# One core, a convolution and dense pair with its gradients: w1's gradient summed with the operands exchanged, products with w2 and the first norm moved forward

## The chip, the cores and the metric

The kernel runs on one core of a Trainium2 chip. Its engines work side by side, each in the order of its own queue: TensorE (PE; its weight loads are shown as PEld), VectorE (DVE), ScalarE (ACT), GpSimd (POOL) and SyncE (SP). Transfers are issued by an engine's queue, mostly SP's and POOL's, and carried out by 16 DMA engines. The metric is the time of one execution on the device in microseconds; the median over runs is compared.

## The reference

Four layers in a row, each on the layer norm of its input `x` (2048 rows of 448), each added to `x`: a long convolution (A), a dense pair (B), A again, B again. All nine results are wanted: the output and the gradients of it for the given `grad_out`.

```python
def _A_ref(q, k, v, shift_k, ssm_k, ssm_D):
    k_shift = ...            # 4 taps along the rows
    kv = k_shift * v
    y_f = rfft(kv, 2*S) * rfft(ssm_k, 2*S)
    y = irfft(y_f)[:S]
    return q * (y + kv * ssm_D)

def _B_ref(x, w1, w2):       # w1 448 x 1792, w2 1792 x 448
    return silu(x @ w1) @ w2

x = A_q
x = x + _A_ref(_layernorm(x), ...)
x = x + _B_ref(_layernorm(x), B_w1, B_w2)
x = x + _A_ref(_layernorm(x), ...)
x = x + _B_ref(_layernorm(x), B_w1, B_w2)
_out, _vjp = jax.vjp(_f, A_q, A_k, A_v, A_shift_k, A_ssm_k, A_ssm_D, B_w1, B_w2)
return (_out, *_vjp(grad_out))
```

Since `y` depends on `k`, `v` and the filter alone, both A layers share one convolution. The gradient of w1 (output 7) is the sum over the 2048 rows, and over both B layers, of the norm that went in (`n3` for the second layer, `n1` for the first) times the gradient at the hidden layer.

## The kernel before

The program has three stages.

*Opening* (`_ssm_prefix`). The filter's spectrum and that of `kv` are made by two stages of 128-wide matmuls. In the loop over `h` and `jq` TensorE convolves the taps (`conv`, `ps_cv`), ScalarE copies `ks`, VectorE multiplies by `v`, and `stage1_kv` makes the first stage of the transform; beside it run the transposes of the filter (`turn`, when `h` is 0) and its second stage (`_fft_stage2` with `cons_ka`, when `h` is 1). `_ln_steps` is a generator: it makes the first norm of chunk 0, one `bn_stats` and `bn_aggr` for each of four row tiles with a `yield` after each, then in one go the reciprocal root on POOL (`rstd`, L279) and four products on ScalarE (`na`, L285). Its last part stands behind the loop (`for _ in ln0: pass`). Then 14 transfers on POOL swap the halves of the filter's spectrum into `KB`, seven more store the spectrum, and SP loads w1. Seven `turn`s transpose the first stage of `kv` (`A1kv` into `A1K`), 16 blocks of 128 x 128 each, copied by ScalarE or VectorE as the balancer `bal` picks. Then, for each of 14 pieces of 1024 columns, `_fft_stage2` and `cons_prod`: two matmuls, a copy (`xs`), the product with the spectrum on VectorE (`pab`, L471), and two pieces later the inverse stage (`ps_v`, 16 matmuls of 128 columns, L235 and L236) and its copy into `B1`. At the end 16 transposes of `gb0` (the first 512 rows of `grad_out`), a copy to `k.gT0`, and eight steps `ps_y` that give `Ysb`, the convolution `y`.

*Main*. Four chunks of 512 rows go through the layers and back. `H` is the product with w1 (`ps_h`), `O` with w2 (`ps_o`), `G` the product of a gradient with w2 transposed (`ps_g`), `N` that with w1 transposed and the norm's gradient (`ps_n`). TensorE's order is the one in which the program issues (`tc.manual_schedule`); strings such as `"OGGOGGOTOT"` in `weave` and `steps` write it out, one letter a step. `G` and `H` make 7 steps of two blocks each through `_products`: 56 matmuls of 512 columns, of which 12 have only 64 contracted rows and stand in pairs, one on each half of the array's rows, since 448 is three and a half times 128. `G` of chunk 0 (`g20`) and of chunk 1 (`g21`) for the last layer need only `grad_out` and so can be issued at any time; before, `g20` makes three steps in the opening of Main and four after the first norms of layer three, `g21` three there and four within chunk 1's `O`.

*Suffix* (`_ssm_suffix`), with `Jobs` issued between its steps. The suffix makes the gradients of the convolution. `Jobs` makes those of w2 and w1 from operands that Main has stored in DRAM (`OP_d`): `load` brings one tile of 128 hidden columns and 2048 rows (`dstat`, 512 KB), `group` sums over 16 row tiles and two layers, and `run(n)` issues n quarters of that. For w1 (`fin_w1`, 14 tiles):

```python
# mms, L995: st is the tile of the hidden layer's gradient, mov the norm
self.nc.tensor.matmul(ps[:, :D], lhsT=st[:, t, :], rhs=mov[:, t, :], ...)
```

So the hidden gradient is stationary, the norm's 448 columns stream, and the sum comes out as 128 hidden columns x 448. Output 7 is 448 x 1792, so `fin_w1` copies the sum (L1104) and `flush`, called one block later, turns it in four transposes (`ps_dt`, L1117), copies it (L1119) and stores it from POOL (L1120).

## Time and profile before

| what | value |
|---|---|
| median of 3 runs | 717.25 us (716.99 to 719.49) |
| the profiled execution | 716.31 us |
| its span, first to last instruction | 714.5 us |
| mean granted TensorE clock | 0.995 |
| TensorE's stretch of w1's sums (`n3m` from 531.9, `n1m` to 662.8) | 448 matmuls in 131 us, with the suffix's between them |
| the first stop of TensorE over 3 us | 66.6 to 70.25 us |

The busy time of an engine is its instructions' time, laid over each other where they overlap; a matmul's recorded length is from its issue to its end, and the next one starts well before that. The price of a matmul in a stream is the distance between the starts. The 40 slices are 17.9 us each; `PEclk` is the clock granted to TensorE, in tenths.

### The profile page before, as it was taken

To read this page: it belongs to the slowest core of one execution; us is meant where nothing else is said; L and a number is where in the kernel's file an instruction comes from. 1 tells how busy PE (TensorE), PEld (TensorE's weight loads), DVE (VectorE), ACT (ScalarE), POOL (GpSimd) and SP (SyncE) were. 2 spreads that over 40 slices of the span, in tenths; PEclk is the share of its full clock that TensorE was granted. 3 is DMA by queue.
4 is the path that set the end of the run, shared out by engine and by line. 5 is a ranking of instruction groups with operands and counts; after the bars stand their busy time and mean duration, and the time that the engine had idled before them with its cause. 6 is when DMAs were issued, how large, how long until landed. Compare 5 with 4: busy or idle time off the path is not lost.

```text
span 714.5 us, 12786 instructions
## 1 busy us (share of the span) xinstructions
PE 689.3 (96%) x5008; PEld 380.9 (53%) x5008; DVE 486.2 (68%) x1106; ACT 444.2 (62%) x582; POOL 123.3 (17%) x208
## 2 busy tenths in 40 slices
PE   6997899999999999999999999999999999999998
PEld 4886654434444444444444444544566666656655
DVE  4788776758887747877279723934258769869790
ACT  3878877686777868778677685132755555545200
POOL 1034420111011100111001100001212223353130
PEclk9999899999999999999999999999999999999999
DMA  9949998659969999499975999089999897879962
GB/s 303 305 146 234 342 287 255 168 139 270 236 146 235 215 240 242 116 243 231 224 179 133 233 229 365 3 187 249 309 413 357 291 343 245 266 274 377 354 181 95
DMA packets 196237, 172.59 MB, mean 242 GB/s; under 512 B 143090, under 2 KB 174194, under 8 KB 195024
## 3 DMA queue, kind: packets, MB, share of 16 engines
q1 hardware_dynamic: 181280, 115.30, 61.3%
q0 software_dynamic: 13344, 52.54, 20.9%
q10 hardware_dynamic: 1552, 3.94, 1.5%
q8 instruction: 39, 0.64, 0.4%
q14 instruction: 22, 0.18, 0.1%
HBM read 73.25 MB, written 60.10 MB: 187 GB/s over the span
## 4 chain that ended last, share of the span: by engine, by line
PE 62%; issue 8%; DVE 5%; ACT 4%; DMA 3%; POOL 2%; POOLq 0%; DVEq 0%; ACTq 0%
PE ps_d L995 12%; PE ps_n L741 12%; PE ps_h L513 11%; PE ps_g L513 10%; PE ps_o L695 7%; PE ps_d L1030 3%; ACT dT L688 2%; DMA ksf<-KS_d 1%; PE ps_t L580 1%; PE ps_gK L1305 1%; PE ps_tr L1211 1%; POOL rstd L279 1%; PE ps_d L1065 1%; PE ps_s L206 1%; DVE n L287 1%
## 5 line engine op out<-in xcount | busy, mean ns | idle before, releaser
L995 PEld LDWEIGHTS <-dstat 128*128 128x128 bf16 x768 | 72.5, 98 | 61.1
L513 PE MATMUL ps_h<-nT,w1sb 128*128 128x512 bf16 (+1 forms) x448 | 97.4, 380 | 2.6 <-ACT dT L678 1.9
L741 PE MATMUL ps_n<-w1T,ghT 128*128 128x448 bf16 x448 | 92.5, 353 | 0.8 <-DVE ghT L866 0.8
L695 PE MATMUL ps_o<-w2sb,aT 128*128 128x448 bf16 x448 | 88.5, 352 | 0.0
L513 PE MATMUL ps_g<-nT,w2T 128*128 128x512 bf16 (+1 forms) x392 | 82.9, 380 | 0.1
L723 ACT CAST ghT<-ps_g 128x512 bf16<-128x512 f32 (+1 forms) x74 | 54.1, 760 | 41.5 <-PE ps_g L513 41.2
L673 ACT ACTIVATE aT<-ps_h 128x512 bf16<-128x512 f32 (+1 forms) x82 | 60.0, 759 | 29.2 <-PE ps_h L513 27.6
L513 PEld LDWEIGHTS <-w1sb 128*128 128x128 bf16 (+1 forms) x448 | 35.5, 97 | 59.7 <-issue 25.4
L741 PEld LDWEIGHTS <-ghT 128*128 128x128 bf16 x448 | 43.2, 98 | 42.3 <-DVE ghT L866 1.7
L695 PEld LDWEIGHTS <-aT 128*128 128x128 bf16 x448 | 43.5, 98 | 40.1
L513 PEld LDWEIGHTS <-w2T 128*128 128x128 bf16 (+1 forms) x448 | 35.4, 97 | 55.1 <-issue 20.8
L915 DVE SCALAR_TENSOR_TENSOR lb_v<-lb_u,n 128x448 bf16<-128x448 bf16 x48 | 30.0, 624 | 46.8 <-ACT lb_u L745 46.3
L279 POOL TENSOR_TENSOR rstd<-ln_ve,mhalf 128x2 f32<-128x2 f32 (+2 forms) x27 | 23.0, 851 | 198.8 <-DVE ln_ve L277 198.8
L688 ACT ACTIVATE dT<-dT 128x1024 bf16<-128x1024 bf16 (+1 forms) x64 | 55.0, 940 | 0.1
L995 PE MATMUL ps_d<-n1m,dstat 128*128 128x448 bf16 x224 | 48.6, 352 | 0.0
L995 PE MATMUL ps_d<-n3m,dstat 128*128 128x448 bf16 x224 | 48.6, 352 | 0.0
L678 ACT CAST dT<-ps_h 128x1024 bf16<-128x1024 f32 (+1 forms) x50 | 42.8, 872 | 0.0
L745 ACT ACTIVATE lb_u<-ps_n,rstd 128x448 bf16<-128x448 f32 x32 | 20.7, 647 | 34.5 <-PE ps_n L741 26.3
L995 PE MATMUL ps_d<-X,dstat 128*128 128x448 bf16 x160 | 34.2, 353 | 0.0
L995 PE MATMUL ps_d<-go,dstat 128*128 128x448 bf16 x160 | 33.7, 353 | 0.0
L581 ACT COPY nT<-ps_t 128x1024 bf16<-128x1024 bf16 x20 | 20.2, 1008 | 18.7 <-PE ps_t L580 18.7
L866 DVE TENSOR_TENSOR ghT<-dT,ghT 128x512 bf16<-128x512 bf16 (+2 forms) x24 | 18.1, 778 | 19.2 <-ACT ghT L723 17.0
(217 smaller groups left out, 1245.1 us busy)
## 6 DMA issues: line engine op xcount, KB each, us to landing
dstat<-g_d SPq DMA_DIRECT2D x28, 512.0 KB, 5.6
dstat<-a_d SPq DMA_DIRECT2D x23, 512.0 KB, 7.1
a_d<-turned SPq DMA_DIRECT2D x16, 512.0 KB, 4.1
g_d<-turned SPq DMA_DIRECT2D x16, 512.0 KB, 3.9
a_d<-turned SPq DMA_DIRECT2D x16, 384.0 KB, 3.3
g_d<-turned SPq DMA_DIRECT2D x16, 384.0 KB, 3.3
N_d<-n POOLq DMA_DIRECT2D x10, 448.0 KB, 4.6
spec_K<-ZK POOLq DMA_DIRECT2D x7, 512.0 KB, 7.7
```

The source lines that it names most:

```text
L279: k.ln_pow = nc.gpsimd.tensor_tensor(out=r[:, lo:hi], in0=ve[:, 0:n], in1=k.mhalf[:, 0:n], op=ALU.pow)
L513: nc.tensor.matmul(ps(u, u + 1)[:, 0, :], lhsT=wT[h, b, ft * P:(ft + 1) * P], rhs=rhs[h, b, :], start=start, stop=stop)
L673: self.last_silu = nc.scalar.activation(aT[hh][:, o:o + hi - lo, :], ps(lo, hi), ACT.Silu)
L678: nc.scalar.copy(self.dpart(dT, 2 * fp + lo, 2 * fp + hi), ps(lo, hi))
L688: self.nc.scalar.activation(d[:, o:o + n, :], d[:, o:o + n, :], ACT.Derivative_silu)
L695: nc.tensor.matmul(po[:, :D], lhsT=aT[ft // 7][:, ft % 7, tl * P:(tl + 1) * P], rhs=self.w2sb[:, ft, :], start=(ft == 0), stop=(ft == NF - 1))
L723: nc.scalar.copy(g, ps(lo, hi))
L741: nc.tensor.matmul(pn[:, :D], lhsT=gh[ft // 7][:, ft % 7, tl * P:(tl + 1) * P], rhs=self.w1T[:, ft, :], start=(ft == 0), stop=(ft == NF - 1))
L745: nc.scalar.activation(u0[:], pn[:, :D], ACT.Identity, scale=k.rstd[2 * L + 1][:, t:t + 1], accum_out=cp[:, tl, 0:1])
L915: nc.vector.scalar_tensor_tensor(out=v[:], in0=u0, scalar=-1.0 / D, in1=n_t, op0=ALU.mult, op1=ALU.mult, accum_out=cp[:, 1:2])
L995: self.nc.tensor.matmul(ps[:, :D], lhsT=st[:, t, :], rhs=mov[:, t, :], start=(first and t == 0), stop=(last and t == NT - 1))
L1030: nc.tensor.matmul(ps[ft][:, :D], lhsT=get(t), rhs=mov[:, t, :], start=ft not in seen, stop=(last[ft] == i and t == hi - 1))
```

## The change

`pair` takes the place of `group`, `fin_w1` and `flush` for w1: it makes two tiles of hidden columns at once, with the norm as the stationary operand and the hidden gradient's 128 columns streaming, so that the sums come out as output 7 wants them. The 448 norm columns are three blocks of 128 and one of 64; the 64-column block of the two tiles goes to the two halves of the array's columns and of one PSUM bank (`ps[0][64 * u:64 * u + 64, 384:512]`). For each row tile it issues block 0 for both tiles, the two narrow ones, and blocks 1 and 2 for both tiles: eight matmuls of 128 columns. It yields after every two row tiles, eight times a layer and pair as before. Each tile's sum is copied once and stored in two transfers. The call to `go2` moves from `group` to the last pair.

In the opening the transposes of `gb0` come before the products with the spectrum; their result lies partly in `gb0`'s own place and partly in `X`. Three steps of chunk 0's `G` (`g_step`) are issued at pieces 6 and 10 and after the last, into `k.gh0`, which lies in the rows of `X` of chunks 2 and 3; `Main.G` takes the same generator on. In Main the patterns change so that `g20` makes its four other steps before the first `H`, and `g21` its seven after the first norms of layer three; chunk 1's `"OGGOGGOTOT"` then finds no `G` step left. `gh0` serves again as the first half of chunk 0's other `G`. `_ln_steps` yields once more, after `rstd`; its steps are taken when `h` is 0 and the rest when `h` is 1. Two of the filter's second-stage pieces move to the end of `h` = 0. The `turn`s of `kv` get a fixed engine, ScalarE for g of 0, 3 and 6. w1's three loads move from SP to POOL, behind the stores of the filter's spectrum, and the memset of `w2T` to the end of the loop.

```diff
@@ -277,6 +277,7 @@
         k.ln_pow = nc.gpsimd.tensor_tensor(out=r[:, lo:hi], in0=ve[:, 0:n], in1=k.mhalf[:, 0:n], op=ALU.pow)
+        yield
         if eng is nc.scalar:
@@ -364,11 +365,11 @@
-        def turn(src, dst, g):
+        def turn(src, dst, g, eng=None):
             pt = psum.tile([P, 16, P], BF16, name="ps_tr", **a_)
...
                 nc.tensor.transpose(pt[:, i, :], src[:, 16 * g + i, :], k.ident[:])
-            _copy(nc, bal.pick(2048, dve_ns=0.53), dst[:, 16 * g:16 * g + 16, :], pt[:])
+            _copy(nc, eng or bal.pick(2048, dve_ns=0.53), dst[:, 16 * g:16 * g + 16, :], pt[:])
@@ -432,11 +433,13 @@
                             turn(A1Kf, Z, g)
+                    next(ln0)
+                    if i == 3:
+                        _fft_stage2(k, Z, psum, cons_ka, range(2))
                 else:
-                    _fft_stage2(k, Z, psum, cons_ka, range((0, 4, 8, 11)[i], (4, 8, 11, 14)[i]))
+                    _fft_stage2(k, Z, psum, cons_ka, range(2 + 3 * i, 5 + 3 * i))
                     next(ln0, None)
-        for _ in ln0:
-            pass
+        nc.gpsimd.memset(k.w2T[0:64, 3, 0:2 * P], 0.0)
         for i in range(7):
@@ -444,9 +447,9 @@
         k.w1sb = k.wk.tile([P, ND, F], BF16, name="w1sb", tag="WB")
-        nc.sync.dma_start(out=k.w1sb[:, 0:3, :], in_=k.B_w1[0:384].rearrange("(c p) f -> p c f", p=P))
-        nc.sync.dma_start(out=k.w1sb[64:128, 3, :], in_=k.B_w1[384:448, :])
-        nc.sync.dma_start(out=k.w1sb[0:64, 3, 2 * P:], in_=k.B_w1[320:384, 2 * P:])
+        nc.gpsimd.dma_start(out=k.w1sb[:, 0:3, :], in_=k.B_w1[0:384].rearrange("(c p) f -> p c f", p=P))
+        nc.gpsimd.dma_start(out=k.w1sb[64:128, 3, :], in_=k.B_w1[384:448, :])
+        nc.gpsimd.dma_start(out=k.w1sb[0:64, 3, 2 * P:], in_=k.B_w1[320:384, 2 * P:])
         nc.gpsimd.memset(k.w1sb[0:64, 3, 0:2 * P], 0.0)
@@ -455,18 +458,46 @@
         for g in range(7):
-            turn(A1f, Zkv, g)
+            turn(A1f, Zkv, g, nc.vector if g % 3 else nc.scalar)
+        bal.reset()
         hold = []
+        k.X = k.wk.tile([P, NT, D], BF16, name="X", tag="WX")
+        Xf = k.X[:].rearrange("p t d -> p (t d)")
+        k.gh0 = Xf[:, 8 * D:].rearrange("p (a s) -> p a s", s=512)
+        pt = psum.tile([P, ND, 512], BF16, name="ps_t", tag="A", bufs=4)
+        for b, (lo, hi) in enumerate(BLK):
+            for tl in range(4):
+                nc.tensor.transpose(pt[:, b, tl * P:(tl + 1) * P], k.gb0[:, tl, lo:hi], k.ident[:])
+        g3 = k.gb0[:].rearrange("p t d -> p (t d)")[:, 0:1536].rearrange("p (b s) -> p b s", s=512)
+        g1 = Xf[:, 4 * D:4 * D + 512].rearrange("p (b s) -> p b s", s=512)
+        nc.vector.tensor_copy(g3, pt[:, 0:3])
+        nc.vector.tensor_copy(g1, pt[:, 3:4])
+        bal.add("dve", 1.3)
+        class Sets:
+            def __getitem__(self, at):
+                h, b, cols = at
+                return g3[h, b, cols] if b < 3 else g1[h, 0, cols]
+        def banks():
+            ps = psum.tile([P, 2, 512], FP32, name="ps_g", tag="A", bufs=4)
+            return lambda lo, hi: ps[:, lo:hi, :]
+        k.banks = banks
+        k.g20 = _products(nc, lambda: k.banks(), k.w2T, Sets())
+        def g_step():
+            fp, ps = next(k.g20)
+            _copy(nc, bal.pick(1024), k.gh0[:, 2 * fp:2 * fp + 2, :], ps(0, 2))
...
             if ci % 2 == 1:
-                st = nc.gpsimd.dma_start(out=k.SPEC_d["KV"][:, (ci - 1) * 1024:(ci + 1) * 1024], in_=Zf[:, (ci - 1) * 1024:(ci + 1) * 1024])
-            if ci == 3:
-                with tc.issue_after(st.ins):
-                    nc.gpsimd.memset(k.w2T[0:64, 3, 0:2 * P], 0.0)
+                nc.gpsimd.dma_start(out=k.SPEC_d["KV"][:, (ci - 1) * 1024:(ci + 1) * 1024], in_=Zf[:, (ci - 1) * 1024:(ci + 1) * 1024])
             pab = work.tile([P, 2, 1024], BF16, name="pab", tag="pab", bufs=3)
@@ -474,19 +505,13 @@
                 _fft_inv_stage2_chunk(k, pa, pb, False, B1, cj, psum)
+            if ci in (6, 10):
+                g_step()
         _fft_stage2(k, Zkv, psum, cons_prod)
-        k.X = k.wk.tile([P, NT, D], BF16, name="X", tag="WX")
-        k.gT0 = k.X[:].rearrange("p t d -> p (t d)")[:, 11 * D:11 * D + 2048].rearrange("p (b t) -> p b t", b=ND)
+        g_step()
         for pa, pb, cj in hold:
             _fft_inv_stage2_chunk(k, pa, pb, False, B1, cj, psum, halves=cj == NCI - 1)
-        pt = psum.tile([P, ND, 512], BF16, name="ps_t", tag="A", bufs=4)
-        for b, (lo, hi) in enumerate(BLK):
-            for tl in range(4):
-                nc.tensor.transpose(pt[:, b, tl * P:(tl + 1) * P], k.gb0[:, tl, lo:hi], k.ident[:])
-        nc.vector.tensor_copy(k.gT0, pt[:])
         B1v = B1.rearrange("p a (c n s) -> p a c n s", c=2, n=16)
@@ -701,12 +726,18 @@
-    def G(self, gT, res, dT=None, dv=()):
+    def G(self, gT, res, dT=None, dv=(), first=None):
         nc, k = self.nc, self.k
         half = lambda h: self.t([P, NF // 2, 512], f"ghT{h}", "T", 5)
-        res[:] = [half(0)]
+        res[:] = [half(0) if first is None else first]
+        if gT is None:
+            k.banks = lambda: self.banks("ps_g")
+            prods = k.g20
+        else:
+            prods = _products(nc, lambda: self.banks("ps_g"), self.w2T, gT)
         gh = res
-        for fp, ps in _products(nc, lambda: self.banks("ps_g"), self.w2T, gT):
+        for fp, ps in prods:
             if fp == 3:
@@ -807,13 +838,13 @@
         gh2 = []
-        g20 = self.G(k.gT0, gh2, dv=(2,))
+        g20 = self.G(None, gh2, dv=(5,), first=k.gh0)
...
-        steps("GGtttG", G=g20, t=self.T2(self.n0[0][1], nT))
+        steps("GGtttGG", G=g20, t=self.T2(self.n0[0][1], nT))
         gb = gb_load(0)
@@ -825,8 +856,8 @@
         g21 = self.G(gT, gh21)
-        steps("GGGG", G=g20)
         next(g20, None)
+        steps("GGGG", G=g21)
         nT = self.nT()
@@ -883,7 +914,7 @@
                 self.fwd1(c + 1, [self.chain] * 4)
-                g = self.G(gT, gh1, dT0)
+                g = self.G(gT, gh1, dT0, first=None if c else k.gh0)
                 if c:
@@ -1009,8 +1039,6 @@
             yield from self.mms(ps[ft], st, movs[0](), 0, NT, True, False)
-        if fts == (12, 13):
-            self.go2()
         for ft in fts:
@@ -1044,9 +1072,8 @@
         movs = (lambda: self.n3, self.n1)
-        for f in range(12):
-            yield from self.group((f,), wkeys, movs, self.fin_w1)
-        yield from self.group((12, 13), wkeys, movs, self.fin_w1)
+        for i in range(NF // 2):
+            yield from self.pair(i, wkeys, movs)
         for f in range(7, 13):
@@ -1096,28 +1122,40 @@
         nc.scalar.copy(o[:], ps[:, :D])
-        self.flush()
         (nc.gpsimd if ft < NF - 2 else nc.sync).dma_start(out=k.outs[8][ft * P:(ft + 1) * P, :], in_=o[:])
-    def fin_w1(self, ft, ps):
-        o = self.out()
-        self.nc.scalar.copy(o[:], ps[:, :D])
-        self.flush()
-        self.pend = (ft, o)
-    def flush(self):
+    def pair(self, i, keys, movs):
         nc, k = self.nc, self.k
-        if self.pend is None:
-            return
-        ft, o = self.pend
-        self.pend = None
-        out7v = k.outs[7].rearrange("(c p) f -> p c f", p=DC)
-        pt = k.psum.tile([DC, ND, P], BF16, name="ps_dt", tag="tr", bufs=1)
-        for dc in range(ND):
-            nc.tensor.transpose(pt[:, dc, :], o[:, dc * DC:(dc + 1) * DC], k.ident[:])
-        o7 = k.dp3.tile([DC, ND, P], BF16, name="do7", tag="do7", bufs=2)
-        nc.scalar.copy(o7[:], pt[:])
-        nc.gpsimd.dma_start(out=out7v[:, :, ft * P:(ft + 1) * P], in_=o7[:])
+        fts = (2 * i, 2 * i + 1)
+        ps = [self.bank(tag) for tag in (("jb", "tr") if i % 2 else ("po", "po"))]
+        for L in range(2):
+            st = [self.load(keys[L], ft) for ft in fts]
+            n = movs[L]()
+            for t in range(NT):
+                last = L == 1 and t == NT - 1
+                for b in range(3):
+                    cols = slice(b * P, (b + 1) * P)
+                    for u in range(2):
+                        nc.tensor.matmul(ps[u][:, cols], lhsT=n[:, t, cols], rhs=st[u][:, t, :], start=(L == 0 and t == 0 and b == 0), stop=(last and b == 2))
+                    if b == 0:
+                        for u in range(2):
+                            nc.tensor.matmul(ps[0][64 * u:64 * u + 64, 384:512], lhsT=n[:, t, 384:D], rhs=st[u][:, t, :], start=False, stop=False)
+                if t % 2:
+                    yield 1
+            if L == 0 and i == NF // 2 - 1:
+                self.go2()
+        out = k.outs[7]
+        for u, ft in enumerate(fts):
+            o = k.dp3.tile([P, 4, P], BF16, name="dout", tag="do7", bufs=2)
+            if u == 0:
+                o0 = o
+            m = 4 - u
+            nc.scalar.copy(o[:, 0:m, :], ps[u][:, 0:m * P].rearrange("p (b f) -> p b f", f=P))
+            cols = slice(ft * P, (ft + 1) * P)
+            nc.gpsimd.dma_start(out=out[0:384, cols].rearrange("(b p) f -> p b f", p=P), in_=o[:, 0:3, :])
+            nc.gpsimd.dma_start(out=out[384:D, cols], in_=o0[64 * u:64 * u + 64, 3, :])
```

More of the change, by code (lines that the diff above doesn't have):

```diff
@@ L1098, in fin_w2 @@
         nc.scalar.copy(o[:], ps[:, :D])
-        self.flush()
         (nc.gpsimd if ft < NF - 2 else nc.sync).dma_start(out=k.outs[8][ft * P:(ft + 1) * P, :], in_=o[:])
-    def fin_w1(self, ft, ps):
-        o = self.out()
-        self.nc.scalar.copy(o[:], ps[:, :D])
-        self.flush()
-        self.pend = (ft, o)
-    def flush(self):
-        nc, k = self.nc, self.k
-        if self.pend is None:
-            return
-        ft, o = self.pend
-        self.pend = None
-        out7v = k.outs[7].rearrange("(c p) f -> p c f", p=DC)
-        pt = k.psum.tile([DC, ND, P], BF16, name="ps_dt", tag="tr", bufs=1)
-        for dc in range(ND):
-            nc.tensor.transpose(pt[:, dc, :], o[:, dc * DC:(dc + 1) * DC], k.ident[:])
-        o7 = k.dp3.tile([DC, ND, P], BF16, name="do7", tag="do7", bufs=2)
-        nc.scalar.copy(o7[:], pt[:])
-        nc.gpsimd.dma_start(out=out7v[:, :, ft * P:(ft + 1) * P], in_=o7[:])
+    def pair(self, i, keys, movs):
+        nc, k = self.nc, self.k
+        fts = (2 * i, 2 * i + 1)
[26 more added lines that the diff above has]
+            nc.gpsimd.dma_start(out=out[384:D, cols], in_=o0[64 * u:64 * u + 64, 3, :])
```

## The prediction

> **What bounds the kernel now.** I read the busy table and the 40 slices first, then the groups by line and form, the chain of waits, busy times by stretch, and last the timeline around single places.
>
> ```profile
> span 714.5 us, 12786 instructions
> PE 689.3 (96%) x5008; PEld 380.9 (53%) x5008; DVE 486.2 (68%) x1106; ACT 444.2 (62%) x582; POOL 123.3 (17%) x208
> PEclk9999899999999999999999999999999999999999
> ```
>
> TensorE is busy 96% of the span, at full clock but for the fifth slice. So what a change does to TensorE's own work is paid one for one, except in the few places where TensorE stands still. Those lie in the opening, here in the timeline of TensorE and then of ScalarE (start, length, count at the end):
>
> ```profile
> 65.14 1.46 PE L217 MATMUL ps_s<-A1K,Gsb 128*128 128x512 bf16 x6
> 70.25 0.29 PE L235 MATMUL ps_v<-Gsb,pab 128*128 128x128 bf16 x1 [3.65 <-DVE pab L471]
> 70.33 0.31 PE L236 MATMUL ps_v<-Gsb,pab 128*128 128x128 bf16 x1
> 70.44 0.31 PE L235 MATMUL ps_v<-Gsb,pab 128*128 128x128 bf16 x1
> ...
> 65.32 2.72 ACT L285 ACTIVATE na<-x0c,ln_nmr,rstd 128x448 bf16<-128x448 bf16 x4
> 67.94 2.81 ACT L111 CAST A1K<-ps_s 128x1024 bf16<-128x1024 f32 x3
> ```
>
> The first product with the spectrum (`pab`) comes late because ScalarE does the first norm's four `na` before the copy that feeds it. After that stop TensorE starts its 128-column matmuls 0.106 us apart, twice the 0.056 seen elsewhere: the clock is down until 75.8. The stretch 71 to 95 shows VectorE busy 19.0 and ScalarE 19.3 of 24 us, TensorE 20.2 in part at half clock: there VectorE and ScalarE set the pace.
>
> Behind the opening TensorE hardly stops. The sums of w1's gradient (`n3m`, `n1m`, L995) run from 532 to 663 between the steps of the suffix. Two groups by form, three pieces of the chain, and a stretch (TensorE's busy time first, then its loads', VectorE's, ScalarE's, POOL's):
>
> ```profile
> L995 PE MATMUL ps_d<-n1m,dstat 128*128 128x448 bf16 x224 | 48.6, 352 | 0.0
> L995 PE MATMUL ps_d<-n3m,dstat 128*128 128x448 bf16 x224 | 48.6, 352 | 0.0
> ...
> 531.20 0.89 PE ps_tr L1211 x16
> 545.58 2.27 PE ps_d L995 x12
> 672.73 0.22 PE ps_dt L1117 x4
> ...
> 532.00:678.00 146.00, 145.92 (x1418) 93.54 (x1415) 114.25 (x235) 72.97 (x93) 44.90 (x76) 1.00 0.88 317
> ```
>
> TensorE is busy 145.92 of 146 us there, so longer sums move the end by their whole length. The means of 352 and 219 ns are latencies; matmuls overlap, so the price is the distance between starts: 2.27/12 = 0.189 us for 448 columns, 0.89/16 = 0.0556 us for 128.
>
> **The change part by part.** *Sums of w1's gradient.* Now: 448 matmuls of 448 columns, 448 x 2.27/12 = 84.8 us, and 14 x 0.22 = 3.1 us of transposes; 87.9 in all. After: for each of 224 steps (7 pairs, 2 layers, 16 row tiles) six full matmuls of 128 columns and two whose stationary side has only 64 columns, one for each half of the array, standing between two full ones and four full ones. The built order has them so: 2 full, 2 narrow, 4 full, and so on. If the two narrow ones run together, a step streams 7 x 0.0556 = 0.389 us, 87.2 in all: no loss. But the trace shows what a passage between a full and a narrow array costs, in TensorE's timeline and in the chain:
>
> ```profile
> 668.42 1.68 PE L995 MATMUL ps_d<-go,dstat 128*128 128x448 bf16 x8
> 670.03 1.08 PE L1318 MATMUL ps_sk<-kx_s,gks 128*32 128x128 bf16 x64
> 671.04 0.74 PE L995 MATMUL ps_d<-go,dstat 128*128 128x448 bf16 x3
> ...
> 334.62 1.73 PE ps_g L513 x8
> 479.62 3.23 PE ps_g L513 x16
> ```
>
> Eight full matmuls from 668.42 should end at 669.93 (8 x 0.189); the narrow ones start at 670.03, 0.10 late. Those 64 are 16 steps of four side by side and should end at 670.92; the next full one starts at 671.04, 0.12 late. Together 0.22 us. The products with w2 say the same of 64-row halves: eight full ones take 1.73 (0.216 each), but sixteen with two pairs of halves, 14 streams or 3.02 us, take 3.23: 0.21 for one trip there and back. So a step costs 0.389 + 0.21 = 0.599 us, and 224 steps 134.2: **+46.3 us** against 87.9. No row has an array of 64 columns. From below, its passage is free: 87.2, so -0.7. From above, the pair doesn't overlap (+224 x 0.056 = +12.5): +58.8. The rows of 32 columns and of 64 rows lie on both sides of it and agree within 0.01 us, so I take theirs, and for the wider load of stationary columns some 10 ns more a step (the row of 112 columns, L1305, loads for 130 ns where others take 98, so 0 to 32 ns), +2.2: **+48.5**.
>
> The Trainium skill, "TensorEngine Tiling (Array Packing)", section Key Properties, says that a change of tiling mode drains the array, and lists 128x64 as a mode of its own; by that the price of the rows holds here too, and no run here has shown this mode.
>
> The new form copies once per block instead of twice (ScalarE 14 x (536 + 598) ns = 15.9 us becomes about 8) and issues 28 stores on POOL instead of 14, 14 x 0.74 = 10.4 us more. From 532 to 678 POOL is busy 45 of 146 us and ScalarE 73: TensorE covers both. Behind these stores stand APart's loads, and VectorE that waits for them; its last work ends at 698, ahead of 714, and each step of the suffix gets longer by the same TensorE time. SP's loads are as many; two tiles are in use at once, of six by then, and TensorE takes longer for each. If TensorE did not cover it, POOL's 10.4 us would be the price.
>
> *Products with w2 sooner.* The number of `ps_g` matmuls stays 392, with the same pairs of halves. Three steps of chunk 0 move into the stretch 66 to 95: 1.73 + 1.93 + 1.30 = 4.96 us of TensorE under VectorE's and ScalarE's pace: **-5.0**. Their price there is three copies of about 1.0 us. The 16 transposes of grad_out (0.9 us) move to where TensorE waited 3.65 us anyway. Then all of chunk 0 is done before the first H and all of chunk 1 at 133 to 141, four steps each, as long as before; so four steps (6.8 us) leave chunk 1's O at 247 to 255, which in the chain are cover for ScalarE's slopes (until 251.0). O and transposes there last 10.6 + 0.9 us from 240.6, to 252; the stop is 0 to 2 us, taken as 0.
>
> *First norm beside the convolution; loads moved.* `na` leaves the place above and goes between the convolution's copies; four statistics (4 x 0.79 us) leave VectorE's fullest stretch (50 to 58: 7.96 of 8), and two copies of Ka move forward, so I take 0 there (-1 to +2.7, all of `na`). The seventh turn goes to ScalarE (1.87 us from 65.3), so the first copy starts at 67.2, not 67.94. From there 14 products x 1.22 us and 31 copies (1.02 on ScalarE, 1.22 on VectorE) balance at 25.0 us a side: 92.2. The same sum before gives 91.3, the trace 95.4: 4.1 us of stops, of which VectorE's wait for the swapped halves (1.66 us at 73) falls away. Its swaps took 9 us to land beside w1's load (issued 57.7, landed 71.1), which now comes behind them and the four last stores of K's spectrum on POOL; at about 75 us and 12 us to land that is 87, ahead of 109. Behind it on POOL wait the stores of the second spectrum, which w2's and w1T's loads wait for (96.7 now); ps_o needs w2 at 120.9. SP loses three issues that nobody queued behind. The stretch ends near 94.6: **-1.2** with the transposes gone from its end. From above the opening gains what TensorE loses there: stops of 9.6 us at 66 to 109 and 2.8 us of half clock, -12.4; from below it pays for copies and `na`, +2.
>
> Sum: +48.5 - 5.0 - 1.2 = +42.3. The profiled execution took 716.31 us (span 714.5, 1.8 around it), which gives 758.6; the median of the three runs is 717.25, 0.9 above it, hence **759 us**.
>
> **Rivals.** *The array's passages cost nothing at 64 columns*, and the change does what its names say: 716.3 - 0.7 - 6.2 = 709.4, 710 at the median. For it: transposes and 14 copies go. Against: some 50 round trips in this trace (three in each of 16 sets of products, four in `ps_sk`), none of those read free. The point from which it decides: with +6.9 us of w1's sums, 0.03 us a step, the opening's gain is spent. 7%. *Half of it is hidden*, as one of the two passages overlaps with the load: +46.3 - 23.5 - 6.2 gives 733. Against: both ways are late by the same 0.10 to 0.12. 4%. *The stream of 128 columns with a load each does not hold 0.056 us*: the trace has only runs of 16 of it unmixed with others; if it took the load's 98 ns, 1344 x 0.042 = +57 on top, 816. Against: `ps_v` and `ps_tr` hold 0.056. 2%. The Trainium skill, "TensorE: Matmul & The Clock Gate", section Back-to-back issue gap, gives 81 ns a matmul for a sustained stream of loads and 128-column matmuls; by that 1344 x 25 ns, an estimate of 34 us, would come on top, 793. The rows here say 56. *The clock goes down* in this stretch, as after the 3.65 us stop: 84 us of streaming twice, 840. Against: the gaps are 0.1 us. 2%.
>
> **How the numbers follow.** The forecast has 85%. Its own range is 749 (0.20 a trip and no slower load, the opening's whole 12.4) to 772 (the pair not overlapping). That holds 8 in 10 of all, as the cases at 710 and 733 and those above have 15%; I give 746 to 772. A measurement here tells 0.5% (3.6 us) from no change. Faster by more: the case at 710, 6%; within: 2%; slower: 92%.
>
> **What would show it.** The narrow matmuls should start 0.15 us after the full one before them, and the next full one some 0.16 after that; the stretch of the `n3m` and `n1m` matmuls should grow from 131 us to about 180 with TensorE at full clock. The first `ps_v` should start near 69.5, none 0.106 apart, and `ps_y` near 94.7. The forecast is wrong if a step of eight takes 0.39 us, or if TensorE stops for longer than 3 us anywhere behind 110.

## The result, and the profile after

The changed kernel takes 759.83 us at the median of four runs (758.1 to 760.67), the kernel before beside it 717.12 (712.58 to 719.49): a ratio of 1.060, with a 95% interval of 1.054 to 1.066. Ratios, here and below, leave out executions that took over 1.5% longer than the fastest of the same kernel. The forecast was 759. The profiled execution took 760.38 us. Its page begins with the span, the busy time of each engine, and the clock granted in 40 slices:

```profile
span 758.6 us, 15330 instructions
PE 733.4 (97%) x6251; PEld 431.4 (57%) x6296; DVE 489.3 (65%) x1108; ACT 437.1 (58%) x566; POOL 133.8 (18%) x225
PEclk9999999999999999999999999999999999999999
```

TensorE has 44.1 us more busy time in a span that is 44.1 us longer (733.4 - 689.3; 758.6 - 714.5). The fifth slice, 8 before, now reads 9 like the others: TensorE's matmuls of 128 columns start 0.06 us apart from the first `ps_v` on. The timeline of TensorE and of ScalarE in the opening:

```profile
66.19 0.59 PE L217 MATMUL ps_s<-A1K,Gsb 128*128 128x512 bf16 x2 [0.20 <-ACT A1K L111]
68.37 0.23 PE L235 MATMUL ps_v<-Gsb,pab 128*128 128x128 bf16 x1 [1.59 <-DVE pab L502]
68.44 0.22 PE L236 MATMUL ps_v<-Gsb,pab 128*128 128x128 bf16 x1
68.49 0.22 PE L235 MATMUL ps_v<-Gsb,pab 128*128 128x128 bf16 x1
...
64.27 1.87 ACT L111 COPY A1K<-ps_tr 128x2048 bf16<-128x2048 bf16 x1 [0.81 <-PE ps_tr L371]
66.04 2.85 ACT L111 CAST A1K<-ps_s 128x1024 bf16<-128x1024 f32 x3
```

The four `na` are gone from between ScalarE's copies, and the stop of 3.65 us has become one of 1.59.

The sums of w1's gradient, by form, and then one stretch of all their matmuls (length; busy time of TensorE, its loads, VectorE, ScalarE and POOL; clock):

```profile
L1141 PE MATMUL ps_d<-dstat,n3m 128*128 128x128 bf16 x672 | 62.7, 221 | 0.3
L1141 PE MATMUL ps_d<-dstat,n1m 128*128 128x128 bf16 x672 | 62.0, 221 | 0.1
L1144 PE MATMUL ps_d<-dstat,n1m 128*64 128x128 bf16 x224 | 27.6, 243 | 0.0
L1144 PE MATMUL ps_d<-dstat,n3m 128*64 128x128 bf16 x224 | 27.6, 243 | 0.0
L1144 PEld LDWEIGHTS <-n3m 128*64 128x64 bf16 x224 | 12.2, 106 | 11.6
```

```profile
524.70:706.50 181.80, 181.43 (x2409) 137.14 (x2414) 112.83 (x233) 63.92 (x74) 51.06 (x86) 1.00 0.68 239
```

The stretch is 181.8 us where it was 130.9, at full clock and with TensorE busy all through. The idle column of the groups is near nothing, and yet the same products take longer: the loss lies in the distances between starts, not in any wait that the profile lists. One step in TensorE's timeline:

```profile
599.86 0.25 PE L1144 MATMUL ps_d<-dstat,n1m 128*64 128x128 bf16 x2
600.04 0.51 PE L1141 MATMUL ps_d<-dstat,n1m 128*128 128x128 bf16 x6
600.48 0.25 PE L1144 MATMUL ps_d<-dstat,n1m 128*64 128x128 bf16 x2
600.66 0.40 PE L1141 MATMUL ps_d<-dstat,n1m 128*128 128x128 bf16 x4
```

From one narrow pair to the next, eight matmuls, it is 0.62 us; seven streams of 0.0556 are 0.389. Six full ones from 600.04 should be done at 600.37, and the pair starts at 600.48; the pair's one stream should end at 600.54, and the next full one starts at 600.66.

Added up start to start over the whole stretch, w1's sums take 139.2 us, against 88.1 before: +51.1. Everything ahead of the suffix has become shorter by 5.6 us. One thing has to be taken out of such a comparison: the first convolution matmul (`ps_cv`) starts anywhere between 22.7 and 27.7 us in the profiles of this study. The first loads end TensorE's wait at 4.2 to 5.4 us, and the recorded clock becomes full at 7.8 us in the profile with the earliest `ps_cv` and at 20.3 us in the one with the latest. It started at 26.19 in the profile before and at 24.55 in the one after. So I compare from the first `ps_cv` on: to the last `ps_n` 476.2 us before and 470.6 after, to the end of the span 688.3 and 734.0. The difference, +45.7, less the 1.6 us of the earlier start, is the 44.1 of the spans.

### The profile page after: what moved, and what is told of

Its sections match the earlier page's. It is cut to its first block, busy times and chain, and to the rows that moved or that the text cites. A ratio compares the mean times of both kernels' runs of the same rounds, so it can differ in the third digit from the quotient of the medians.

```text
span 758.6 us, 15330 instructions
## 1 busy us (share of the span) xinstructions
PE 733.4 (97%) x6251; PEld 431.4 (57%) x6296; DVE 489.3 (65%) x1108; ACT 437.1 (58%) x566; POOL 133.8 (18%) x225
## 4 chain that ended last, share of the span: by engine, by line
PE 80%; DVE 5%; issue 5%; ACT 5%; DMA 3%; POOL 2%; SPq 0%; POOLq 0%
PE ps_d L1141 13%; PE ps_n L772 11%; PE ps_g L538 10%; PE ps_h L538 9%; PE ps_d L1025 8%; PE ps_o L720 7%; PE ps_d L1144 5%; PE ps_d L1058 2%; PE ps_v L235 2%; PE ps_v L236 2%; PE ps_s L206 2%; DMA ZK<-ZK 1%; PE ps_t L605 1%; POOL rstd L279 1%; DVE n L288 1%
## 5 line engine op out<-in xcount | busy, mean ns | idle before, releaser
L720 PE MATMUL ps_o<-w2sb,aT 128*128 128x448 bf16 x448 | 88.3, 352 | 0.1
L772 PE MATMUL ps_n<-w1T,ghT 128*128 128x448 bf16 x392 | 81.5, 353 | 0.8 <-DVE ghT L897 0.8
L538 PE MATMUL ps_g<-nT,w2T 128*128 128x512 bf16 (+1 forms) x378 | 80.9, 380 | 1.1 <-issue 0.5
L754 ACT CAST ghT<-ps_g 128x512 bf16<-128x512 f32 (+1 forms) x65 | 47.2, 752 | 36.7 <-PE ps_g L538 36.4
L1141 PE MATMUL ps_d<-dstat,n3m 128*128 128x128 bf16 x672 | 62.7, 221 | 0.3
L1141 PE MATMUL ps_d<-dstat,n1m 128*128 128x128 bf16 x672 | 62.0, 221 | 0.1
L772 PEld LDWEIGHTS <-ghT 128*128 128x128 bf16 x392 | 37.8, 98 | 37.3 <-DVE ghT L897 1.7
L1025 PEld LDWEIGHTS <-dstat 128*128 128x128 bf16 x320 | 30.7, 98 | 28.4 <-issue 0.7
L1141 PEld LDWEIGHTS <-n3m 128*128 128x128 bf16 x672 | 39.8, 98 | 10.7
L1141 PEld LDWEIGHTS <-n1m 128*128 128x128 bf16 x672 | 39.4, 98 | 9.2
L111 ACT CAST B1v<-ps_v 128x1024 bf16<-128x1024 f32 x14 | 14.2, 1012 | 45.5 <-PE ps_v L236 45.5
```

Source lines behind the costliest of these rows:

```text
L538: nc.tensor.matmul(ps(u, u + 1)[:, 0, :], lhsT=wT[h, b, ft * P:(ft + 1) * P], rhs=rhs[h, b, :], start=start, stop=stop)
L720: nc.tensor.matmul(po[:, :D], lhsT=aT[ft // 7][:, ft % 7, tl * P:(tl + 1) * P], rhs=self.w2sb[:, ft, :], start=(ft == 0), stop=(ft == NF - 1))
L754: nc.scalar.copy(g, ps(lo, hi))
L772: nc.tensor.matmul(pn[:, :D], lhsT=gh[ft // 7][:, ft % 7, tl * P:(tl + 1) * P], rhs=self.w1T[:, ft, :], start=(ft == 0), stop=(ft == NF - 1))
L1141: nc.tensor.matmul(ps[u][:, cols], lhsT=n[:, t, cols], rhs=st[u][:, t, :], start=(L == 0 and t == 0 and b == 0), stop=(last and b == 2))
```

## Experiments

Two questions: is the price of w1's sums that of the passages between full and narrow array, and where do the 5.6 us ahead of the suffix come from? In the table, each time is the difference of two starts in the trace of one profiled execution; ratios are of the timed runs to those of the kernel before on the same chip, with 95% intervals. Experiments 1 to 3 and 5 ran on one chip, 4 and 6 to 8 on a second, 9 to 12 on a third.

| kernel | first `ps_cv` to first `ps_y` | to last `ps_n` | w1's sums | ratio |
|---|---|---|---|---|
| before | 69.70 | 476.19 | 88.1 | 1 |
| after | 69.86 | 470.64 | 139.2 | 1.060 [1.054, 1.066] |
| 1: w1's sums alone | 69.86 | 476.25 | 139.2 | 1.073 [1.069, 1.077] |
| 2: all but w1's sums | 69.83 | 470.60 | 88.3 | 0.996 [0.994, 0.999] |
| 3: 16 narrow pairs together | 69.86 | 470.60 | 93.5 | 0.999 [0.996, 1.003] |
| 4: 2 narrow pairs together | 69.86 | 470.60 | 113.8 | 1.025 [1.022, 1.029] |
| 5: no narrow ones | 69.85 | 470.60 | 101.6 | 1.012 [1.008, 1.015] |
| 6: as 2, w1 loaded by SP | 69.83 | 470.66 | 88.9 | 0.992 [0.990, 0.995] |
| 7: as 2, no products in the opening | 66.81 | 471.90 | 88.6 | 0.995 [0.992, 0.997] |
| 8: as 2, norm where it was | 73.43 | 474.39 | 89.1 | 0.996 [0.994, 0.998] |
| 9: as 2, neither of 7 and 8 | 67.56 | 473.33 | 89.5 | 1.000 [0.998, 1.002] |
| 10: as 2, products' copies twice | 70.58 | 471.51 | 88.9 | 0.999 [0.996, 1.002] |
| 11: as 2, products' matmuls twice | 72.82 | 473.61 | 88.6 | 0.998 [0.997, 1.000] |
| 12: as 2, copies on ScalarE | 69.75 | 470.56 | 88.8 | 0.995 [0.992, 0.997] |

The stretch up to `ps_y` is the same within 0.03 us in all six profiles whose opening is that of the changed kernel or differs in w1's load alone, so there a difference of 0.5 us is told apart that the timed runs, with their differing starts, cannot tell.

### The two halves of the change apart (1 and 2)

Experiment 1 is the kernel before with the new `pair` alone; 2 is the changed kernel with `group`, `fin_w1` and `flush` back.

```diff
# 1, in the kernel before; 2 is the reverse in the kernel after
 class Jobs:
-    def group(...), fin_w1(...), flush(...)
+    def pair(self, i, keys, movs):
```

> The kernel before with the new sums of w1's gradient alone. If the passages between full and narrow array are the loss (224 round trips of 0.228 us in the trace after, on top of 87.2 us of streaming, against 88.1 before), it takes 717.1 + 51 = 768 us. If the opening's moves have a part in the loss, less than 760.

> The changed kernel with the old sums of w1's gradient. If the span's remainder (44.1 us longer, of which the sums make 51) is the opening's gain, it takes 717.1 - 7 = 710 us. If the new sums won something behind themselves, it stays at 717.

They measured 765.73 us (763.91 to 767.83) and 712.13 (708.39 to 720.43), with 714.21 for the kernel before. The stretches show the sums at 139.16 us with the old opening as with the new, and 470.60 with the new opening whatever the sums do: ahead of the suffix the two parts don't touch each other, and the whole of the loss is in the sums.

Experiment 2 was expected at 7 us below the kernel before and came out only 2.1 below. The suffix of its profile shows much of why. From the last `ps_n` to the end of the span the kernel before takes 212.2 us and experiment 2 takes 216.2, so that of the 5.6 us won ahead of it only 1.6 arrive at the end (686.8 us from the first `ps_cv`, for 688.3). TensorE's longest waits there in experiment 2 are for the tiles of `Jobs` and for VectorE's products; the kernel before has none over 0.24 us:

```profile
PE ps_d L1026 <- DMA dstat<-a_d: 1.7, 2, 0.9
PE ps_v L236 <- DVE pb L1273: 1.0, 2, 0.6
```

In the changed kernel, with its longer sums, the suffix takes only 0.2 us more than with the same sums behind the old opening (263.4 and 263.2), and so nearly all of the 5.6 us arrives there. In the other seven changed kernels with the old sums (6 to 12) it is 0.9 to 2.4 us longer than before, which is why their ratios say less of the opening than the stretches do.

### What the sums pay for (3, 4 and 5)

Experiments 3 and 4 issue as many matmuls of each kind as the changed kernel, but the narrow ones of 16 (or 2) row tiles one after the other: 14 (or 112) round trips in place of 224. Experiment 5 has no narrow ones: the last 64 norm columns are done as a full block of columns 320 to 447, whose upper half is stored.

```diff
# 3; for 4, 16 and 15 are 2 and 1
-                    if b == 0:
-                        for u in range(2):
-                            nc.tensor.matmul(ps[0][64 * u:64 * u + 64, 384:512], lhsT=n[:, t, 384:D], rhs=st[u][:, t, :], ...)
+                    if b == 0 and t % 16 == 15:
+                        for tt in range(t - 15, t + 1):
+                            for u in range(2):
+                                nc.tensor.matmul(ps[0][64 * u:64 * u + 64, 384:512], lhsT=n[:, tt, 384:D], rhs=st[u][:, tt, :], ...)
# 5
-                for b in range(3):
+                for b, (lo, hi) in enumerate(BLK):
...
-                        nc.tensor.matmul(ps[u][:, cols], lhsT=n[:, t, cols], rhs=st[u][:, t, :], ...)
+                        nc.tensor.matmul(ps[u][:, cols], lhsT=n[:, t, lo:hi], rhs=st[u][:, t, :], ...)
```

> The changed kernel, with the narrow matmuls of all 16 row tiles of a layer issued together: the same matmuls, 14 round trips instead of 224. If a passage is the price: 210 x 0.228 = 47.9 us less, 712 us. If the price goes with the number of matmuls and loads, or the two narrow ones don't overlap, it stays near 760.

> The changed kernel with the last 64 columns of the norm taken as a full block of 128 (columns 320 to 447, half of it computed twice): as many matmuls and loads, none narrow. If a passage is the price: 1792 x 0.0556 = 99.6 us of sums instead of 138.4, so 759.8 - 38.8 = 721 us. If many short matmuls with a load each are the price, it stays near 760.

> The 64-column matmuls of two row tiles are issued together, so 112 round trips between the full and the narrow array in place of 224; as many matmuls as the changed kernel. If the price is a fixed 0.228 us a round trip (51.1 us over 224 in the trace), this is 112 x 0.228 = 25.5 us faster than the changed kernel: ratio to the kernel before about 1.025. If the price hangs on each narrow matmul (its own load and stream), nothing is saved: 1.06. If the narrow ones of one tile after the other also pay 0.1 us each, some 10 us are saved: 1.045.

They measured 715.56 us (experiment 3), 722.26 (5), both beside 714.21, and 736.26 (4) beside 717.68. Without the stops at places where TensorE waits for ScalarE (0.78 us after, 0.78 in 4, 1.98 and 0.78 in 3), the sums take 138.4, 113.0 and 90.7 us. From 224 trips to 112 that is 0.227 us a trip, from 112 to 14 (113.0 - 90.7) / 98, again 0.227. What is left at no trips is 87.5, and 1568 streams of 0.0556 are 87.2. So the price is one of passages, the same for each, and neither of the narrow matmuls nor of the 128-column stream. Experiment 5 says the same: eight full matmuls a step, 99.6 us of streams, took 101.6 (1.6 of it at two such stops), 37.6 less than the changed kernel with seven streams' worth. In TensorE's timeline of experiment 3 the passage stands by itself:

```profile
530.67 0.61 PE L1141 MATMUL ps_d<-dstat,n3m 128*128 128x128 bf16 x8
531.21 1.08 PE L1145 MATMUL ps_d<-dstat,n3m 128*64 128x128 bf16 x32
532.23 0.40 PE L1141 MATMUL ps_d<-dstat,n3m 128*128 128x128 bf16 x4
```

Eight full ones from 530.67 are done at 531.11, and the narrow ones begin at 531.21; 16 pairs of 0.0556 are done at 532.10, and the next full one begins at 532.23: 0.10 and 0.13 us for the two ways, where the changed kernel's step with 2 narrow matmuls showed 0.11 and 0.12. In experiment 4 there are four of them, and the two ways again cost 0.10 and 0.12:

```profile
600.68 0.61 PE L1141 MATMUL ps_d<-dstat,n3m 128*128 128x128 bf16 x8
601.22 0.30 PE L1145 MATMUL ps_d<-dstat,n3m 128*64 128x128 bf16 x4
601.45 0.23 PE L1141 MATMUL ps_d<-dstat,n3m 128*128 128x128 bf16 x1
```

The weight loads show a little more of what happens at a passage. Within a run of full matmuls the load of the next one starts 0.05 us ahead of it, beside the matmul before. The loads of the narrow pair at 600.48 in the changed kernel start with their own matmuls, 2 ns ahead:

```profile
600.48 0.11 PEld L1144 LDWEIGHTS <-n1m 128*64 128x64 bf16 x2
```

The load of the full matmul behind them starts 4 ns ahead of it. So at both ways the load is held back together with its matmul; what it waits for, the trace does not name.

Experiment 3 came out 3.6 us above what was expected of it. Against experiment 2, with the same opening, its sums are 5.2 us longer: 14 x 0.227 = 3.2 us are trips that are left, and 2.0 a stop where the suffix waits for a copy of ScalarE's. By these prices no order of the narrow ones makes this form better than the old one by more than 0.9 us (87.2 against 88.1).

### What shortened the part ahead of the suffix (6 to 12)

All of these are experiment 2 with one part undone, or one cost doubled.

```diff
# 6
-        nc.gpsimd.dma_start(out=k.w1sb[:, 0:3, :], ...)
...
+        nc.sync.dma_start(out=k.w1sb[:, 0:3, :], ...)
...
# 7
-            if ci in (6, 10):
-                g_step()
...
-        g_step()
...
-        steps("GGtttGG", G=g20, ...)
+        steps("GGtttGGGGG", G=g20, ...)
# 8; 9 is 7 and 8 together
-                    next(ln0)
-                    if i == 3:
-                        _fft_stage2(k, Z, psum, cons_ka, range(2))
                 else:
-                    _fft_stage2(k, Z, psum, cons_ka, range(2 + 3 * i, 5 + 3 * i))
+                    _fft_stage2(k, Z, psum, cons_ka, range((0, 4, 8, 11)[i], (4, 8, 11, 14)[i]))
                     next(ln0, None)
+        for _ in ln0:
+            pass
```

> The changed opening and Main with w1's sums as before, but w1's three loads stand on SP's queue as in the kernel before, ahead of the swaps. If the swaps of K's halves are late because they share the DMA engines with w1's load (9 us to land in the kernel before), VectorE's wait of some 1.7 us for them comes back and the first ps_y comes at 71.0 to 71.5 us after the first ps_cv in place of 69.8. If the swaps are late anyway, or the wait is covered, it stays at 69.8 within 0.4.

> The changed opening and Main with w1's sums as before, but without the three product steps of chunk 0 in the opening: all seven are issued ahead of the first H. If the three steps (4.96 us of TensorE) lay free under VectorE's and ScalarE's pace in the opening, this is 5.0 us longer from the first ps_cv to the last ps_n than the version with them (470.6 us there), so 475.6, and the opening up to the first ps_y takes the same 69.8 us. If their three copies cost the opening 1.5 us, its first ps_y comes at 68.3 us and the whole is 474.1. If the opening is set by TensorE, it shortens by 5 and nothing changes: 470.6.

> The changed opening and Main with w1's sums as before, but the first norm's steps and the pieces of the second stage of the filter are ordered as in the kernel before. If moving the norm's four products on ScalarE brought what the prediction gave it, the first product with the spectrum comes later by up to 1.9 us and from the first ps_cv to the last ps_n it takes 471.3 to 472.5 us in place of 470.6. If the norm only moves the same ScalarE work from one full place to another, it stays at 470.6 within 0.4.

They measured 712.85, 714.0 and 715.02 us beside 717.68. *w1's load* is worth nothing: 69.83 with either queue. In 6 the swaps take 10.3 us to land beside w1's load, as long as before (9.2), but POOL no longer waits 2.7 us for `na` before it can issue the last of them; in 9 the norm is late but w1 waits, and the swaps land in 4.7. Either change alone takes VectorE's wait away.

*The products* cost the opening 3.0 of their 5.0 us: 66.81 without them, 69.83 with them; to the last `ps_n` they bring 1.3. What they cost, copies or TensorE, the next three tell.

```diff
# 10
-            _copy(nc, bal.pick(1024), k.gh0[:, 2 * fp:2 * fp + 2, :], ps(0, 2))
+            eng = bal.pick(1024)
+            for _ in range(2):
+                _copy(nc, eng, k.gh0[:, 2 * fp:2 * fp + 2, :], ps(0, 2))
# 11, steps 0 and 1 of k.g20; the second pass starts the sums anew
-    for u in range(2):
+    for u in (0, 1, 0, 1):
         for b in range(ND):
             mm(A, 0, u, b, ...)
# 12
-            _copy(nc, bal.pick(1024), k.gh0[:, 2 * fp:2 * fp + 2, :], ps(0, 2))
+            _copy(nc, nc.scalar, k.gh0[:, 2 * fp:2 * fp + 2, :], ps(0, 2))
+            bal.add("act", 1.02)
```

> The changed opening and Main with w1's sums as before; each of the three product steps of chunk 0 in the opening is copied out twice, by the same engine. The three steps cost the opening 3.0 us (first ps_cv to first ps_y 69.83 with them, 66.82 without). If their copies on VectorE and ScalarE are what cost it, three more (two of 1.22 us on VectorE, one of 1.01 on ScalarE) bring some 2.4 to 3 us more: first ps_y near 72.5. If it is the 5 us of TensorE in the chain that cost it, nothing more than 0.5 us comes on top: 69.8 to 70.3.

> The changed opening and Main with w1's sums as before; 14 of the full product matmuls of the first two steps in the opening are issued twice (14 x 0.216 = 3.0 us more of TensorE). If VectorE and ScalarE set the pace and TensorE's products lie beside them, the first ps_y stays within 0.7 us of 69.83 us after the first ps_cv. If a product step stands in the chain ahead of the next pieces, so that VectorE and ScalarE run dry behind it, it comes 2 to 3 us later: 71.8 to 72.8.

> The changed opening and Main with w1's sums as before; the three copies of the product steps in the opening all go to ScalarE (before two of them to VectorE), and the balance between the two is told so. If VectorE's copies are the price of the products in the opening, the first ps_y comes 0.5 to 1.5 us earlier than 69.83. If the balance just hands VectorE other copies instead, or TensorE is the limit, it stays within 0.4.

Three more copies (3.45 us of VectorE and ScalarE) cost 0.75 us of the stretch, and 3.0 us more of matmuls cost 2.99. So around experiment 2 an added matmul on TensorE is paid one for one, and an added copy by a fifth. Experiment 12 tells nothing of VectorE's share: the balancer gave it two other copies for the two that it lost (VectorE is busy 23.05 us of the stretch there and 22.88 in experiment 2), and the stretch stayed within 0.08. How the 3.0 us between experiments 7 and 2 themselves divide between the matmuls and their copies was not measured. VectorE's timeline around the first step, first in experiment 2, then in 11:

```profile
75.25 2.40 DVE L502 TENSOR_TENSOR pab<-A1K,ZK 128x2048 bf16<-128x2048 bf16 x2
78.22 1.22 DVE L112 CAST X<-ps_g 128x1024 bf16<-128x1024 f32 x1 [0.57 <-PE ps_g L538]
79.70 1.23 DVE L502 TENSOR_TENSOR pab<-A1K,ZK 128x2048 bf16<-128x2048 bf16 x1 [0.25 <-ACT A1K L111]
81.53 1.23 DVE L502 TENSOR_TENSOR pab<-A1K,ZK 128x2048 bf16<-128x2048 bf16 x1 [0.61 <-ACT A1K L111]
```

```profile
76.04 3.53 DVE L502 TENSOR_TENSOR pab<-A1K,ZK 128x2048 bf16<-128x2048 bf16 x3
81.86 1.23 DVE L112 CAST X<-ps_g 128x1024 bf16<-128x1024 f32 x1 [2.30 <-remote]
```

While TensorE makes the step, no new piece comes to ScalarE and VectorE, and VectorE, the supposed pacemaker, stands still: 1.43 us around one step, and 2.30 ahead of the copy where the step is doubled (there the view names no releaser, but the copy reads `ps_g`). From the first `ps_v` to the first `ps_y` the busy times (length; TensorE, loads, VectorE, ScalarE, POOL) are, in experiment 7 and then in 2:

```profile
70.73:93.75 23.02, 17.99 (x244) 14.36 (x248) 20.33 (x18) 20.00 (x22) 6.42 (x12) 1.00 0.94 349
```

```profile
68.78:94.82 26.04, 23.24 (x270) 16.47 (x271) 22.88 (x20) 20.95 (x23) 5.95 (x11) 1.00 0.86 304
```

TensorE had 5.0 us free without the products and 2.8 with them, so only part of the 5.0 took up the steps.

*The norm.* Experiment 9, with neither part, was to complete the four combinations of products and norm.

> The changed opening and Main with w1's sums as before, with neither the products in the opening nor the norm beside the convolution; what stays of the change are the transposes ahead, the fixed engines of the turns, w1 on POOL and the two chunks' products ahead of H. First ps_cv to last ps_n took 476.2 us in the kernel before, 470.6 with both, 471.9 with the norm alone, 474.4 with the products alone. If the two parts add up, this takes 475.7, and the rest of the change brings 0.5. If the gain needs both together, it takes 474.5 or less.

It measured 716.1 us beside 717.02, and 473.33 to the last `ps_n`, which by the second of these would mean that the gain needs both parts together. But that reading leans on the 474.4 of experiment 8, and this does not bear it. TensorE's timeline in 8, and then in 9, which has the same instructions up to here:

```profile
68.35 0.59 PE L217 MATMUL ps_s<-A1K,Gsb 128*128 128x512 bf16 x2 [0.39 <-ACT A1K L111]
70.11 0.59 PE L217 MATMUL ps_s<-A1K,Gsb 128*128 128x512 bf16 x2 [1.17 <-ACT A1K L111]
72.29 0.29 PE L235 MATMUL ps_v<-Gsb,pab 128*128 128x128 bf16 x1 [1.58 <-DVE pab L501]
72.37 0.31 PE L236 MATMUL ps_v<-Gsb,pab 128*128 128x128 bf16 x1
72.47 0.31 PE L235 MATMUL ps_v<-Gsb,pab 128*128 128x128 bf16 x1
```

```profile
67.17 0.59 PE L217 MATMUL ps_s<-A1K,Gsb 128*128 128x512 bf16 x2 [0.39 <-ACT A1K L111]
68.94 0.59 PE L217 MATMUL ps_s<-A1K,Gsb 128*128 128x512 bf16 x2 [1.17 <-ACT A1K L111]
71.11 0.23 PE L235 MATMUL ps_v<-Gsb,pab 128*128 128x128 bf16 x1 [1.58 <-DVE pab L501]
71.17 0.22 PE L236 MATMUL ps_v<-Gsb,pab 128*128 128x128 bf16 x1
71.23 0.22 PE L235 MATMUL ps_v<-Gsb,pab 128*128 128x128 bf16 x1
```

The stops are the same, but behind them one execution runs at half clock (0.106 us apart, until 78.3) and the other at full clock. So 8's 474.39 holds a loss that its kernel does not always have. Its stretch from the first `ps_v` to the first `ps_y`, beside that of experiment 2 above, gives the size:

```profile
72.29:101.17 28.88, 25.73 (x266) 18.78 (x271) 22.91 (x20) 21.23 (x23) 7.54 (x14) 0.90 0.86 299
```

VectorE and ScalarE have the same 20 and 23 instructions as there and are busy about as long, and yet the stretch is 2.8 us longer, one more sign that TensorE sets its pace. Without these 2.8 us experiment 8 would take some 471.5 us to the last `ps_n`, an estimate, and inside what was expected of it. By this estimate the products bring 1.8 us with the norm late and 1.3 with it early, and the two parts add up to within 0.5 us. Between executions at full clock, the norm's move is worth 1.4 us (473.33 to 471.90, 9 to 7). The half clock comes on top where it strikes. Of the executions of the kernel before that the ratios of the three sets of runs rest on, 63 of 71 have a mean granted clock of 0.998 or less, of experiments 8 and 9, 12 of 24, and of 2, 6 and 7 only 2 of 25. Within experiment 8 the seven of these have a median of 715.55 us and the five at full clock 713.83, 1.7 us apart, but the two groups overlap (714.65 to 718.39 and 710.36 to 716.91). The Trainium skill, "TensorE: Matmul & The Clock Gate", Part 1, says that activity is judged in windows that run freely, not from the kernel's start, so that the point of a clock change differs from run to run; equal stops with unequal clocks fit that, though no run here shows the windows.

So the 5.6 us are: 2.9 from the kernel before to experiment 9, 1.4 for the norm, 1.3 for the products. Of the 2.9, 2.1 are won up to the first `ps_y` (69.70 to 67.56) and 0.7 behind it, in Main. How much of the 2.1 is the half clock of the profile before (it has it, 9's has not), how much the swaps and how much the transposes is not told apart: the part was not split further.

## Why the prediction was right, point by point

*w1's sums, +48.5.* Measured +51.1. The mechanism was right in each of its steps: the pair runs together (its two starts are 3 ns apart), full matmuls of 128 columns hold 0.0556 us, and each step pays one round trip. Its size was 0.227 us where the forecast had 0.21 and 0.01 for the wider load: start to start, the two ways hold 0.217 beyond the stream, and the first full matmul behind them holds 0.066 in place of 0.056. The way in came at 0.149 us after the full matmul, as foretold (0.15); the way out at 0.176, not 0.16. So the rows of 32 columns and of 64 rows, which lie on both sides of this shape, gave its price within 8%. The rule of the Trainium skill that was set beside it ("TensorEngine Tiling (Array Packing)", Key Properties: a change of mode drains the array) agrees with the traces here as far as each change to 128x64 has a price, 0.227 us there and back, though no view shows the drain itself; the 81 ns that "TensorE: Matmul & The Clock Gate", Back-to-back issue gap, gives for a sustained stream did not show, at 87.5 us left for 1568 streams.

*Copies and stores.* As foretold, next to nothing: POOL is busy 51 of 181.8 us, and the stretch of experiment 1 is 181.8 us as well, with TensorE never idle in it. Behind the last pair TensorE waits 0.6 us for ScalarE's copy of the sum (`dout`), which the sum of terms did not have.

*Products, -5.0, and the norm, -1.2.* Together -5.6 for the -6.2 forecast, but each was wrong and the errors cancelled. The step that failed is "there VectorE and ScalarE set the pace", from which 4.96 us of TensorE were taken as hidden. Main did lose them (from the first `ps_y` to the last `ps_n` 400.8 us for 406.5), but the opening, forecast to end 1.2 us earlier, took as long as before: 3.0 us of the products were paid there, which leaves 1.3 to 2.0 of gain. What hid this was the rest: without the products, experiment 7 is 4.3 us ahead of the kernel before, and 2.9 of them are in the opening, from norm, clock, swaps and transposes, over twice the 1.2. The other 1.4 are in Main, where four steps of chunk 0 that come before the first `H` fill two stops of 0.54 and 0.55 us that TensorE had there, 1.1 of the 1.4. The forecast's sign for the opening, `ps_y` near 94.7, seemed to be met with 94.41, but only because that execution began 1.6 us earlier than the one before.

*w1's load behind the swaps.* Foretold as what takes VectorE's wait away; it does, but the earlier norm alone does so too, and so its move brings nothing here.

*The total.* That the median came within 1 us of the forecast is luck. From the first `ps_cv` on the change costs 45.7 us where the sum had 42.3, and in the two profiled executions the start of `ps_cv`, which no term of it covers, hid 1.6 of the difference. The sums are 2.6 us over the forecast. Two small readings were off and change nothing: TensorE's stops from 66 to 109 us come to 8.5 us, not 9.6, and VectorE's last work ends at 697.0, not 698.

*Chunk 1's O without cover.* Taken as 0 to 2 us, at 0; from 236 to 256 us TensorE's only stop is the same 0.5 us (`ps_h` for a copy) as before.

The rivals: free passages and half-hidden ones fell with experiments 3 and 4, where every trip costs the same. A stream of 128 columns that doesn't hold 0.056 us fell with experiment 5. The clock stayed at 1.00 through the stretch.

The version that beats both is experiment 2, the change without its sums: 0.996 of the time before [0.994, 0.999], a small part of the 5.6 us since its suffix is longer. Experiments 6 and 12 (0.992 and 0.995) differ from it by no more than their intervals.

## What to carry to other kernels

Count passages between array shapes, not only streamed columns: a pair of narrow matmuls between full ones paid 0.227 us on top of 0.056 of work, and putting sixteen pairs together took 46 of the 51 us back. Idle time of an engine in a busy table is no room for work: double the work that is to be hidden and see whether the stretch grows, as a doubled product step did here by its whole 3.0 us and doubled copies by 0.75. When a forecast fits, test its terms one by one, for two wrong ones can give a right sum. And follow a gain to the end of the kernel: 5.6 us won early shrank to 1.6 where later stages were not ready.

## What was not expected of the hardware

The way from the narrow to the full array takes longer than the way in: 0.176 us start to start against 0.149, where 0.056 is the unhindered distance. With two or more narrow pairs (experiments 3 and 4) the last step is 0.152, and the missing 0.02 stands between the first pair and the second, which start 0.08 us apart; the price of the whole trip is the same. The same stops of 0.39, 1.17 and 1.58 us were followed by half clock in one execution and by full clock in another; in all three profiles with a half clock there (before, 1 and 8) it lasts 6.8 us. And the first matmul of the convolution starts between 22.7 and 27.7 us from one execution to the next, a spread of 5.1 us beside the 5.6 that the change wins ahead of the suffix; in the 13 profiles that record it, the later the clock becomes full (7.8 to 20.3 us), the later this start, but for neighbours within 0.4 us of each other.
